# Cutting GpSimd's casts, products and masks into smaller instructions, together with a new order of the opening and fewer idle matrix products

## The chip, the cores and the metric

The kernel runs on one core of one Trainium2 chip. The metric is the device time of one execution in microseconds (us), and lower is better. A core has TensorE (PE in the profile; its weight loads are PEld), VectorE (DVE), ScalarE (ACT), GpSimd (POOL) and SyncE (SP), which here only starts transfers. In the traces the instructions of an engine run one after another (GpSimd's cast of q at 10.00 us stood behind that of a v tile at 9.42, though q was there at about 6.3, as the prediction works out), and the engines run beside each other (in the kernel before, PE, DVE, ACT and POOL are busy for 158.1, 144.6, 129.9 and 112.9 us of a span of 172.9). VectorE and GpSimd also hold each other up. In the kernel before, a cast of VectorE that takes 0.75 us elsewhere took 1.61 at 61.66, beside a cast of GpSimd, and GpSimd's next one 1.58 instead of 1.15. I call what VectorE's casts and masks wait for the port; that is a name for these waits.

## The reference, cut to what matters

```python
# q, k, v: (8, 8, 576, 64); w_in: (512, 1024); A_log: (512,); w_out: (512, 512)
scores = q @ k.transpose(0, 1, 3, 2) / sqrt(64)
scores = where(|i - j| <= 32, scores, -1e9)            # window of 65 positions
x = (softmax(scores) @ v)  -> (8, 576, 512)
val, gate = split(x @ w_in)                            # first projection
h[t] = exp(A_log)[0] * h[t-1] + val[t]                 # scan along the sequence
out = (silu(gate) * h) @ w_out                         # second projection
```

## The kernel before

Five strings (one for each engine) hold the order of the work as letters; further strings say which engine takes each shared piece. A small model of the engines assigns buffers, and `emit` writes the instructions. These are the parts that the change touches.

```python
SEQ = {"pe": "QKBmSKQSmSmSPPKtQVmSPPVm...", "pool": "vqkmavqwwwakwavvvmff...", ...}   # cut
SHARED = {"ck": "GDAGADGDGDGAGAGA", "mask": "pGppppGpDpppDpGpGDDDGD...", ...}        # G, D, A: the engine; cut

def keep_busy(seq, place, until):          # idle products: nobody reads their result
    ...
        n = int((o.start - max(at[b], 5.6 if first else 0.0) - (0.6 if first else 0.15))
                / (0.43 if first else 0.216))
    ...
# in emit(o), e being the engine of the piece
        elif kd in ("cq", "ck"):           # cast of a q or k tile, 128 x 1152, f32 -> f16
            copy(e, bf(n + "16", b, T).rearrange("p j y d -> p y j d"), bf(n, b, T))
        elif kd == "mask":                 # zero what lies outside the window, 128 x 1024
            for h in (slice(0, 2),) if e == "dve" else (slice(0, 1), slice(1, 2)):
                (nc.vector if e == "dve" else nc.gpsimd).tensor_tensor(
                    out=pr[:, h], in0=pr[:, h],
                    in1=m[:, None, :].to_broadcast([128, h.stop - h.start, 512]), op=ALU.mult)
        elif kd == "fuse":                 # silu(gate) * h, 128 x 512
            ...
                eng.tensor_tensor(out=bf("fu", c)[:, x, :], in0=bf("h", *key), in1=bf("si", *key), op=ALU.mult)
```

The softmax here doesn't subtract the row's maximum and nothing guards it: scores larger than these inputs give would overflow.

Of the kernel before, what the change touches and what calls it, by code (L numbers as in the profile page):

```python
# [10 lines left out]
ALU = mybir.AluOpType  # L11
# [6 lines left out]
HALVED = (0, 1, 8)  # L18
# [29 lines left out]
          "fev", "O": "out"}  # L48

SEQ = {  # L50
    "pe": "QKBmSKQSmSmSPPKtQVmSPPVmSQtKGGSmGSPPVVtGPPVGKtVGQGKFFQVmSSQVKFGFFmSPPmSmSSFPPtFKPPtK"
          "QVGmSSSVFGSPPGtVQtVGVPPKGQVQVSSSGFKFtGPPGFKtVSSPVGGQGKFSSPFFGPPSVQttVSSPFVKVQGFFFPSS"
          "VGPPFVQKGFVGPSSVGVVFGGQKVGPPPFFFSSSFFFFPPSVGVGPPVVGGtGGVVGVFGFFVFFFFFF",
    "act": "bvAExhxkxTexqxwxTEggxhvgxhhTkggwEwgegEooqxxevEoogoxxxovxoEvEevxgxxogqgxTTegvEgeexxgo"
           "xoEkggoEvxxqggegExoxooqxgeTkxoxEegvvoooxqgoxEgoegxgkxgogeEgovooxxooxooxggggggogogooo"
           "oo",
    "dve": "eqkavehEwrrnnEwhvhsrrnnwsesuvshurnrnssurnrnssuuTskusssuesvsssmvhvhurrnnkmrnrTnrnrTns"
           "hhsukrnrnuusmsurrnnsussmhmhuTrrnnuuTsrmnuusuvhhmrnrnrnsuTsrnsmsuvmhrhnsrurnnsusussru"
           "nsuusrnrvurnnhmmhmrnrmnsurrsnnususTususssussuussfoo",
    "pool": "vqkmavqwwwakwavvvmffwfqwfqffkvffkqvvmfmfqqvkvffvvmfffkvfmvvmfmfqffvvmkffmfqfmmfvffvv"  # L60
            "ffffffff",
    "sp": "LLLLLLLLLLLLLLLLLLLLLLLLLLLLLLLLLLLLLLLLLLLLLLLLLLLLLLLLLLLLLOLLLLLLLLOLLOLOOLLLLOLL"
          "OLOOOOOXOXLLOLOLLOLXXOOXOOOOOOOOOOOOOOOOOOO",
}
SHARED = {
    "cw": "DDGGDGAGGAAG",
    "ar": "DGGG",
    "ck": "GDAGADGDGDGAGAGA",
    "evk": "ADDAAAAAAAAAAAAA",
    "cq": "GDGAGGAGAGGAAGAG",  # L70
    "evq": "DDADADAAAAAAAAAA",
    "cv": "AGDGDDGGGAADDGDAAGGAAGGGGGAGGDGADAGGAGDG",
    "sh": "ADDDDAAADDDDDDDDDDDD",
    "mask": "pGppppGpDpppDpGpGDDDGDGDGGDDGGGGDDDD",
    "xe": "AAADDDAADDDAD",
    "fuse": "GGGGGGGGGGGGGGGGGGGGGGGGGGGGGGGGGGGD",
    "fev": "AAAAAAAAAAAAAAAAAAAAAAAAAAAAAAAAADAAD",
}
ORDER = ["q00", "v00", "a", "k00", "v01", "q01", "k01", "v02", "q10", "k10", "w00", "w02",
         "v03", "w01", "w03", "q11", "v04", "w11", "k11", "w12", "w10", "w13", "v10", "v11",  # L80
         "v12", "v14", "v13", "w23", "k20", "w20", "q20", "w21", "w22", "k21", "q21", "q30",
         "k30", "v21", "v23", "v20", "v22", "v24", "v30", "k31", "k40", "q31", "v31", "v32",
         "v33", "v34", "k41", "q40", "k50", "q50", "q41", "v40", "v41", "v42", "v51", "v43",
         "v44", "k51", "q61", "k60", "q51", "v52", "v50", "k61", "v53", "v54", "q60", "v63",
         "v62", "v60", "v61", "q70", "v64", "k70", "q71", "k71", "v74", "v72", "v70", "v71",
         "v73"]
ORDER = [(x[0],) + tuple(int(y) for y in x[1:]) for x in ORDER]


# [258 lines left out]
def keep_busy(seq, place, until):  # L348


    span, got = {}, {}
    for o in seq:
        for k in o.use:
            p, i = place[o.n, k]
            if p in ("ps1", "ps2"):
                lo, hi = span.get((k, i, p), (o.start, o.end))
                span[k, i, p] = min(lo, o.start), max(hi, o.end)
    t, first = 3.0, True
    for o in seq:
        if o.eng != "pe" or o.start > until or o.kind in ("mask", "ta") and first:  # L360
            continue
        at = [max([t] + [hi for (k, i, p), (lo, hi) in span.items()
                         if lo < o.start and (b == i or p == "ps2" and b == i + 1)]) for b in range(8)]
        b = min(range(8), key=lambda b: at[b])
        n = int((o.start - max(at[b], 5.6 if first else 0.0) - (0.6 if first else 0.15)) / (0.43 if first else 0.216))
        if n > 0:
            got[o.n] = [b] * n
        t, first = o.start + COST["pe", o.cost][0], False
    return got
# [3 lines left out]
def kernel(  # L373
# [10 lines left out]
    nc = tc.nc  # L384
# [21 lines left out]
    mask = T([128, 8, 64], f16, "mask")  # L406
# [56 lines left out]
    def two(ap):  # L463
        return ap.rearrange("p (i t) -> p i t", i=2)

    def emit(o):
# [49 lines left out]
        elif kd in ("cq", "ck"):  # L516
            b, T = key
            n = kd[1]
            copy(e, bf(n + "16", b, T).rearrange("p j y d -> p y j d"), bf(n, b, T))
        elif kd in ("trq", "trk"):  # L520
            b, T = key
            n = kd[2]
# [48 lines left out]
        elif kd == "mask":  # L571
            m = mask.rearrange("p r q -> p (r q)")
            pr = bf("pr", *key)
            for h in (slice(0, 2),) if e == "dve" else (slice(0, 1), slice(1, 2)):
                (nc.vector if e == "dve" else nc.gpsimd).tensor_tensor(  # L575
                    out=pr[:, h], in0=pr[:, h], in1=m[:, None, :].to_broadcast([128, h.stop - h.start, 512]), op=ALU.mult)
        elif kd == "pv":
            u, G = key
            pr, pv = bf("pr", *key), bf("pv", *key)
# [23 lines left out]
        elif kd == "xe":  # L603
            u, = key
            copy(e, bf("xT", u // 2)[:, u % 2].rearrange("p a t -> p (a t)"), bf("xt", u).bitcast(f16))
        elif kd == "xd":
            u, = key
            nc.sync.dma_start_transpose(out=bf("xT", u // 2)[:, u % 2].rearrange("p a (r t) -> p (a r) t", r=2),
                                        in_=bf("x16", u).rearrange("p a r h d -> p (a r h d)"))
        elif kd in ("pjv", "pjg"):  # L610
            c, x = key
            pj, xT, oc = bf(kd, *key), bf("xT", c), 0 if kd == "pjv" else 4
            if c in HALVED:
                parts = [(pj[:, 256 * i:256 * i + 256], oc + 2 * (x % 2) + i, 256 * (x // 2), 256) for i in range(2)]
            else:
                parts = [(pj, oc + x, 0, 512)]
            for to, w, t0, n in parts:
                for fc in range(4):
                    nc.tensor.matmul(out=to, lhsT=w_in16[:, fc, 128 * w:128 * w + 128],  # L619
                                     rhs=xT[:, t0 // 256:(t0 + n) // 256, fc, :], start=(fc == 0), stop=(fc == 3))  # L620
        elif kd == "scan":
            c, x, cc = key
            lo, n, t0 = (256 * (cc % 2), 256, 256 * (x // 2)) if c in HALVED else (0, 512, 0)
            before = prior(c, x, cc)
            init = bf("h", *before[0])[:, before[1]:before[1] + 1] if before else 0.0
            a0 = 512 - 64 * c + t0
            nc.vector.tensor_tensor_scan(out=bf("h", c, x)[:, lo:lo + n], data0=arep[:, cc, a0:a0 + n],  # L627
                                         data1=bf("pjv", c, x)[:, lo:lo + n], initial=init, op0=ALU.mult, op1=ALU.add)
        elif kd == "tanh":
            nc.scalar.activation(bf("th", *key), bf("pjg", *key), AF.Tanh, bias=0.0, scale=0.5)  # L630
        elif kd == "silu":
            nc.vector.scalar_tensor_tensor(out=bf("si", *key), in0=bf("th", *key), scalar=1.0,  # L632
                                           in1=bf("pjg", *key), op0=ALU.add, op1=ALU.mult)
        elif kd == "fuse":
            c, x = key
            eng = nc.gpsimd if e == "pool" else nc.vector
            if c in HALVED:
                i, t0 = 2 * (x % 2), 256 * (x // 2)
                eng.tensor_tensor(out=bf("fu", c)[:, i:i + 2, t0:t0 + 256], in0=two(bf("h", *key)), in1=two(bf("si", *key)),  # L639
                                  op=ALU.mult)  # L640
            else:
                eng.tensor_tensor(out=bf("fu", c)[:, x, :], in0=bf("h", *key), in1=bf("si", *key), op=ALU.mult)  # L642
        elif kd == "fin":
            c, tt = key[:2]
            cols = slice(256 * key[2], 256 * key[2] + 256) if len(key) > 2 else slice(0, 512)
            fo, fu = bf("fo", *key)[:, cols], bf("fu", c)
            for cc in range(4):
                nc.tensor.matmul(out=fo, lhsT=fu[:, cc, 128 * tt:128 * tt + 128],  # L648
                                 rhs=w_out16[:, cc, cols], start=(cc == 0), stop=(cc == 3))
        elif kd == "fev":  # L650
            cols = slice(256 * key[2], 256 * key[2] + 256) if len(key) > 2 else slice(0, 512)
            copy(e, bf("o", *key)[:, cols], bf("fo", *key)[:, cols])
        elif kd == "out":
            c, tt = key[:2]
            cols = slice(256 * key[2], 256 * key[2] + 256) if len(key) > 2 else slice(0, 512)
            r0 = 512 * c + 128 * tt
            nc.sync.dma_start(out=out_flat[r0:r0 + 128, cols], in_=bf("o", *key)[:, cols])
# [37 lines left out]
```

## Time and profile before

The median of three runs was 173.91 us (173.71 to 174.9). The profiled execution took 174.91, one us more than the median, for a span of 172.9.

| what | before |
|---|---|
| PE busy / GpSimd busy / GpSimd's instructions | 158.1 us / 112.9 us / 125 |
| one whole product on GpSimd (L642, L639) | 1.16 to 1.21 us |
| half a mask on GpSimd (L575) | 1.19 us |
| granted clock of TensorE | 1.00 in all slices; the clock records begin at 16.25 us |

The prediction below shows the busy row and the first three stages. The columns are the stretch, its length, and the busy us and number of instructions of PE, PEld, DVE, ACT and POOL, then granted clock, share of the DMA engines and GB/s.

### The profile page before, as it was taken

The page shows a single profiled execution, that of the slowest core. Times are in us where ns is not written, and L with a number is a line of the kernel's source. Part 1 is how long each engine was busy: PE and PEld are TensorE (multiplying, and loading weights), DVE is VectorE, ACT ScalarE, POOL GpSimd, SP SyncE. Part 2 cuts the span into 40 slices and gives each one's busy share as a digit, 9 for nine tenths or more (in the row PEclk, how much of TensorE's full clock was granted, in tenths as well). Part 3 has the DMA queues.
Part 4 walks back from the last instruction along what each step waited for, and adds up shares of the span by engine and source line. Part 5 has one row for each costly group of instructions (what it writes and reads, how often), then busy time and mean ns, then how long its engine had stood idle before and what let it go on. Part 6 is the DMA issues. An engine that isn't in the chain of part 4 may idle for free. (4 is left out here: it accounts for less than half of the span.)

```text
span 172.9 us, 5244 instructions
## 1 busy us (share of the span) xinstructions
PE 158.1 (91%) x2133; PEld 99.2 (57%) x2133; DVE 144.6 (84%) x237; ACT 129.9 (75%) x171; POOL 112.9 (65%) x125
## 2 busy tenths in 40 slices
PE   0949788998999998999999999999999999999991
PEld 0225466867967666566666565654654555458650
DVE  5117879988999999899999898979967997899970
ACT  3103849899899997999999999999696869522541
POOL 8560399669657192299949976992999990045520
PEclk9999999999999999999999999999999999999999
DMA  4999998999999979999899998991889428189155
GB/s 122 300 348 372 334 336 154 226 308 383 311 215 227 335 161 298 379 211 230 255 358 254 256 285 181 345 394 74 142 219 306 114 61 186 34 279 357 62 223 202
DMA packets 58574, 42.53 MB, mean 246 GB/s; under 512 B 44084, under 2 KB 44344, under 8 KB 58552
## 3 DMA queue, kind: packets, MB, share of 16 engines
q1 hardware_dynamic: 58552, 42.22, 84.8%
q8 instruction: 16, 0.26, 0.6%
q14 instruction: 6, 0.05, 0.1%
HBM read 31.46 MB, written 9.44 MB: 236 GB/s over the span
## 5 line engine op out<-in xcount | busy, mean ns | idle before, releaser
L619 PE MATMUL psum<-xT,w_in 128*128 128x256 f16 (+1 forms) x384 | 69.9, 326 | 0.4 <-ACT xT L449 0.4
L619 PEld LDWEIGHTS <-w_in 128*128 128x128 f16 x384 | 35.6, 98 | 21.0 <-issue 0.6
L627 DVE TENSOR_TENSOR_SCAN f2k<-arep,f2k,psum 128x512 f32<-128x512 f32 (+1 forms) x44 | 44.2, 1025 | 2.8 <-PE psum L619 2.7
L575 POOL TENSOR_TENSOR pr<-pr,mask 128x512 f16<-128x512 f16 x24 | 28.0, 1187 | 23.2 <-ACT pr L565 20.8
L565 ACT ACTIVATE pr<-psum 128x1024 f16<-128x1024 f32 x36 | 36.4, 1028 | 3.5 <-PE psum L560 3.2
L642 POOL TENSOR_TENSOR fu<-f2k,si 128x512 f16<-128x512 f32 x24 | 28.9, 1214 | 13.2 <-DVE rc L590 9.0
L648 PE MATMUL psum<-w_out,fu 128*128 128x512 f16 (+1 forms) x148 | 34.6, 373 | 0.1
L630 ACT ACTIVATE th<-psum 128x512 f16<-128x512 f32 x36 | 21.5, 605 | 8.7 <-PE psum L619 7.2
L449 ACT ACTIVATE f2k<-psum 128x512 f32<-128x512 f32 (+1 forms) x35 | 20.2, 604 | 9.9 <-PE psum L648 8.4
L632 DVE SCALAR_TENSOR_TENSOR si<-th,psum 128x512 f16<-128x512 f16 x36 | 23.8, 674 | 3.5 <-ACT th L630 3.2
L595 DVE TENSOR_TENSOR x<-psum,rc 128x512 f16<-128x512 f32 x36 | 23.8, 680 | 0.5
L648 PEld LDWEIGHTS <-fu 128*128 128x128 f16 x148 | 13.9, 98 | 13.7
L639 POOL TENSOR_TENSOR fu<-f2k,si 128x512 f16<-128x512 f32 x11 | 12.7, 1159 | 10.3 <-DVE si L632 6.5
L449 ACT ACTIVATE kT<-psum 128x1152 f16<-128x1152 f16 x14 | 15.9, 1138 | 2.1 <-PE psum L525 2.1
L662 PE MATMUL psum<-eye,ident 128*128 128x512 f16 x34 | 12.1, 491 | 5.3 <-POOL eye L434 4.2
L456 POOL TENSOR_SCALAR vE<-v 128x512 f16<-128x512 f32 x20 | 12.7, 643 | 4.2 <-DMA v<-in_v_dram 4.0
L586 PEld LDWEIGHTS <-pr 128*64 128x64 f16 x576 | 11.5, 111 | 6.5 <-issue 5.2
L449 ACT ACTIVATE qT<-psum 128x1152 f16<-128x1152 f16 x12 | 13.7, 1140 | 0.6 <-PE psum L525 0.5
L525 PE MATMUL psum<-ident,q 128*128 128x128 f16 x144 | 11.2, 225 | 3.0 <-POOL q L456 3.0
L560 PEld LDWEIGHTS <-kT 64*128 64x128 f16 x576 | 10.5, 95 | 5.8 <-issue 4.1
L586 PE MATMUL psum<-vO,pr 128*64 128x65 f16 x256 | 13.1, 197 | 0.8 <-DVE vO L452 0.5
L586 PE MATMUL psum<-vE,pr 128*64 128x65 f16 x320 | 13.6, 197 | 0.2
(65 smaller groups left out, 195.9 us busy)
## 6 DMA issues: line engine op xcount, KB each, us to landing
stg<-in_q_dram SPq DMA_DIRECT2D x16, 576.0 KB, 8.3
stg<-in_k_dram SPq DMA_DIRECT2D x16, 576.0 KB, 6.6
out_dram<-f2k SPq DMA_DIRECT2D x35, 256.0 KB, 3.8
v<-in_v_dram SPq DMA_DIRECT2D x24, 256.0 KB, 6.5
v<-in_v_dram SPq DMA_DIRECT2D x16, 192.0 KB, 5.1
f2k<-in_moe_w_in_dram SPq DMA_DIRECT2D x8, 256.0 KB, 8.8
f2k<-in_moe_w_out_dram SPq DMA_DIRECT2D x4, 256.0 KB, 7.0
out_dram<-f2k SPq DMA_DIRECT2D x2, 128.0 KB, 1.9
```

Source lines behind the costliest of these rows:

```text
L449: nc.scalar.activation(dst, src, AF.Copy, bias=0.0, scale=mul)
L456: nc.gpsimd.tensor_scalar(out=dst, in0=src, scalar1=mul, scalar2=1.0, op0=ALU.mult, op1=ALU.mult)
L565: nc.scalar.activation(bf("pr", *key), bf("sc", *key), AF.Exp, bias=0.0, scale=1.0 / 8.0)
L575: (nc.vector if e == "dve" else nc.gpsimd).tensor_tensor(out=pr[:, h], in0=pr[:, h], in1=m[:, None, :].to_broadcast([128, h.stop - h.start ...
L586: nc.tensor.matmul(out=pv[p0:p0 + 64, h, x0:x0 + 65], lhsT=pr[:, h, at:at + 64], rhs=vt, start=True, stop=True)
L595: nc.vector.tensor_tensor(out=x, in0=view[:, :, :, 0:64], in1=bf("rc", *key)[:, :, :, None].to_broadcast([128, 2, 4, 64]), op=ALU.mult)
L619: nc.tensor.matmul(out=to, lhsT=w_in16[:, fc, 128 * w:128 * w + 128], rhs=xT[:, t0 // 256:(t0 + n) // 256, fc, :], start=(fc == 0), stop=( ...
L627: nc.vector.tensor_tensor_scan(out=bf("h", c, x)[:, lo:lo + n], data0=arep[:, cc, a0:a0 + n], data1=bf("pjv", c, x)[:, lo:lo + n], initial ...
L630: nc.scalar.activation(bf("th", *key), bf("pjg", *key), AF.Tanh, bias=0.0, scale=0.5)
L632: nc.vector.scalar_tensor_tensor(out=bf("si", *key), in0=bf("th", *key), scalar=1.0, in1=bf("pjg", *key), op0=ALU.add, op1=ALU.mult)
L642: eng.tensor_tensor(out=bf("fu", c)[:, x, :], in0=bf("h", *key), in1=bf("si", *key), op=ALU.mult)
L648: nc.tensor.matmul(out=fo, lhsT=fu[:, cc, 128 * tt:128 * tt + 128], rhs=w_out16[:, cc, cols], start=(cc == 0), stop=(cc == 3))
```

## The change

It has three parts. GpSimd's q and k casts and its products are issued as two instructions and its masks as four; the intention was that VectorE, where it has to wait at the port, waits for a shorter instruction. The order of the work is new; the opening is what it was meant to speed up, but the strings differ to their ends. And fewer idle products are issued.

```diff
 SEQ = {
-    "pe": "QKBmSKQSmSmSPPKtQVmSPPVmSQtKGG..."
+    "pe": "mQBKQKKSSSmSQPPmmSPSPKttVVmQmV..."        (all five strings, SHARED and ORDER: cut)
-        n = int((o.start - max(at[b], 5.6 if first else 0.0) - (0.6 if first else 0.15)) / (0.43 if first else 0.216))
+        n = int((o.start - max(at[b], 5.6 if first else 0.0) - (0.6 if first else 0.3)) / (0.43 if o.start < 20.0 else 0.216))
@@ cast of q and k
-            copy(e, bf(n + "16", b, T).rearrange("p j y d -> p y j d"), bf(n, b, T))
+            to, src = bf(n + "16", b, T).rearrange("p j y d -> p y j d"), bf(n, b, T)
+            for y in (slice(0, 1), slice(1, 2)) if e == "pool" else (slice(0, 2),):
+                copy(e, to[:, y], src[:, y])
@@ mask
             for h in (slice(0, 2),) if e == "dve" else (slice(0, 1), slice(1, 2)):
+                for x in (slice(0, 512),) if e == "dve" else (slice(0, 256), slice(256, 512)):
@@ product
+            for i in (slice(0, 2),) if e == "dve" else (slice(0, 1), slice(1, 2)):
+                ...
+                eng.tensor_tensor(out=to, in0=two(h)[:, i], in1=two(si)[:, i], op=ALU.mult)
```

## The prediction

> **What bounds the kernel now.** I read the page's busy row first, then the table of busy time by stage, the same table for the idle products alone (L662, matrix products whose result nobody reads[...]), then the chain of waits, then the timelines of GpSimd, TensorE and VectorE around the places that those pointed to. The first fence is the page's busy row and the stage table (columns: stretch, its length, then busy us of PE, PEld, DVE, ACT, POOL); the second is the stage table of L662 alone.
>
> ```profile
> PE 158.1 (91%) x2133; PEld 99.2 (57%) x2133; DVE 144.6 (84%) x237; ACT 129.9 (75%) x171; POOL 112.9 (65%) x125
> 0.00:16.50 16.50, 9.71 (x39) 4.27 (x41) 6.65 (x23) 3.31 (x5) 8.54 (x21) 1.00 0.90 284
> 16.50:30.00 13.50, 11.17 (x220) 7.79 (x220) 10.55 (x17) 10.01 (x10) 9.77 (x12) 1.00 1.03 280
> 30.00:75.00 45.00, 43.34 (x725) 31.60 (x722) 42.57 (x68) 41.62 (x55) 27.26 (x30) 1.00 0.98 283
> 75.00:169.30 94.30, 93.87 (x1167) 55.52 (x1159) 84.47 (x131) 74.92 (x103) 67.30 (x64) 1.00 0.77 219
> ```
>
> ```profile
> 0.00:16.50 16.50, 7.15 (x16) 2.08 (x16) 1.00 0.90 284
> 16.50:30.00 13.50, 3.50 (x14) 1.22 (x13) 1.00 1.03 280
> 30.00:75.00 45.00, 1.42 (x5) 0.36 (x5) 1.00 0.98 283
> 75.00:169.30 94.30, 0.00 (x0) 0.00 (x0) 1.00 0.77 219
> ```
>
> TensorE is the bound. Its useful work is about 158.1 - 12.1 = 146.0 us, and it ends at 169.3, so 23.3 us of TensorE's time are lost, all of it idle or spent on idle products. By stage the loss is 16.5 - (9.71 - 7.15) = 13.9 us before 16.5, then 13.5 - (11.17 - 3.50) = 5.8, then 45 - (43.34 - 1.42) = 3.1, then 0.4. From 75 us to the end nothing can be won except by arriving there with more work done. After 169.3 an eviction and the last transfer take the remaining 3.6 us of the 172.9 us span; the timed run is about 1 us above the span. The chain of waits agrees: from 121.9 us on it is TensorE alone.
>
> ```profile
> 121.91 1.02 PE psum L648 x4
> ...
> 164.89 4.34 PE psum L648 x24
> 169.23 0.02 issue
> 169.25 0.42 DVE f2k L452
> ```
>
> So the change is worth what it takes from the 19.7 us lost before 30 us and from the 3.1 us after them. Why is the opening slow? The next fence is GpSimd's timeline, the one after it TensorE's.
>
> ```profile
> 9.42 0.62 POOL L456 TENSOR_SCALAR vE<-v 128x512 f16<-128x512 f32 x1 [2.62 <-DMA v<-in_v_dram]
> 10.00 1.15 POOL L456 TENSOR_SCALAR q<-stg 128x1152 f16<-128x1152 f32 x1
> 11.12 1.15 POOL L456 TENSOR_SCALAR k<-stg 128x1152 f16<-128x1152 f32 x1
> ```
>
> ```profile
> 11.21 1.14 PE L525 MATMUL psum<-ident,q 128*128 128x128 f16 x9 [2.59 <-POOL q L456]
> 14.84 1.72 PE L662 MATMUL psum<-eye,ident 128*128 128x512 f16 x4
> 16.48 0.41 PE L560 MATMUL psum<-qT,kT 64*128 64x64 f16 x16
> ```
>
> The first q tile was asked for before the first v tile, and ScalarE took that v at 6.29, so q was there at about 6.3; yet its cast began at 10.00, because GpSimd runs in order and stood in front of a v tile until 9.42. That is 3.7 us lost at the very start. Also, ScalarE had the first kT out at 14.53 + 1.12 = 15.65, but the first scores started at 16.48: the idle products before them, 0.43 us each at the slow clock, overran by 0.8 us.
>
> The second subject is the port. The next fence is VectorE's timeline at 60 us, then GpSimd's.
>
> ```profile
> 61.66 1.61 DVE L452 CAST k<-stg 128x1152 f16<-128x1152 f32 x1
> 63.20 1.62 DVE L575 TENSOR_TENSOR pr<-pr,mask 128x1024 f16<-128x1024 f16 x1
> ```
>
> ```profile
> 61.51 1.15 POOL L456 TENSOR_SCALAR k<-stg 128x1152 f16<-128x1152 f32 x1
> 62.70 1.58 POOL L456 TENSOR_SCALAR q<-stg 128x1152 f16<-128x1152 f32 x1
> ```
>
> The cast of 0.75 us (as at 13.67) took 1.61, ending 0.6 after GpSimd's instruction ended at 62.66; the mask of 0.69 took 1.62, ending half a us after GpSimd's next.
>
> [...] Here nine transposes took 1.14 at 11.21 and 0.68 at 16.82, so the clock came up some 5.5 us after work began[...]; the granted-clock column reads 1.00 throughout and does not show this.
>
> **The change part by part.**
> Counting letters in the diff, TensorE's useful instructions are the same: 146 us stay. VectorE gets two more masks, one more shift, one more arep and one more q cast, and loses two k casts, two weight casts and a v cast: 2 x 0.69 + 0.7 + 0.7 + 0.75 - 2 x 0.75 - 2 x 0.42 - 0.42 = +0.8 us. ScalarE gets four q/k casts and one weight cast more, three v casts and one shift less: 4 x 1.17 + 0.63 - 3 x 0.63 - 1.07 = +2.3 us on an engine 75% busy.
>
> Splitting: GpSimd's casts took 0.622 us for 512 elements and 1.152 for 1152, a slope of 0.83 ns and a fixed part of about 0.2 us; back to back, starts are 0.04 closer than durations, so a cut costs about 0.16 us (I take the same for products). Cuts: 35 products, 13 casts, 10 masks with two each, 68 in all, x 0.16 = +10.9 us. The moved work is two masks (-4.5), three q casts (-3.5), one arep (-1.2), four v casts (+2.3) and one weight cast (+0.6) = -6.3. GpSimd goes from 112.9 to about 117.5 us, 68%: still not a bound. A product comes 0.16 us later; in the last stage it is followed by TensorE work that is already queued, so little of it reaches the end.
>
> What the cuts give: I added, over VectorE's timeline, how much each cast, shift or mask exceeded its usual 0.42, 0.75, 0.70 or 0.69. Fifteen were long, by 6.6 us in all, 2.5 of it between 25 and 33 us. Waits end with GpSimd's current instruction, so halved instructions should about halve them: 3.3 us of VectorE back. Nearly all of this falls beside a TensorE that is already full after 75 us. Before that, TensorE has 3.1 us to regain between 30 and 75; I allow 0.5, and charge 0.3 for the later products.
>
> The opening: k, q, k, q, k, q now come first and v afterwards. In 3.13 us (6.29 to 9.42) 832 KB landed, 272 GB/s. The first q is now second in the queue, behind a k: 576 + 576 KB where before 576 + 192 KB were in at 6.29, so it lands near 7.5. VectorE casts it (0.75), TensorE transposes at about 8.3, against 11.21. ScalarE then evicts it (1.13), and only after that casts the first k (1.17), which I read from its order; transpose (1.1) and VectorE's eviction (1.36) put the first kT at about 14.5. Two more k halves are transposed before the scores, so these start at about 16, close to 16.48, but with three scores in a row. v and the weights land later: up to the fourth first-projection weight the old order has 5.4 MB in front, the new one 6.5, some 3 us more, so 24.5 against about 21. The first projection was at 26.65; following the engines by hand I get 26.3. Before it the new order has one k transpose (0.5), two scores (0.8), two products with v (0.86), one x transpose (0.45) and a mask (0.2) more: 2.8 us of useful work that the old order did later. I count 2.0 of it, because this hand schedule assumes that each landing is on time. The overrun of the idle products, 0.8, is inside this.
>
> Sum: -2.0 - 0.5 + 0.3 = -2.2 us, and 173.9 - 2.2 = 171.7; fewer idle products late in the opening may add 0.2. I say 171.5.
>
> **The rivals.**
> First: the opening is limited by DMA and the lead evaporates. For it: the DMA share is 1.03 from 16.5 to 30[...]. Then projections wait and the time is 173 to 174. Against it: the attention work that can run meanwhile is there.
> Second: VectorE becomes the bound after 30 us. It was busy 42.57 of 45 there, so a TensorE 2.5 us ahead may wait for it. That eats the lead: 173. Against it: [...]there are 10 us of slack after 75.
> Third: everything works, and the 3.1 us between 30 and 75 go too: 2.8 + 2 us, 169.2.
> Fourth: fewer idle products let the clock fall again in the opening[...]. Against it: useful products are denser.
>
> **Range and chances.** The first two rivals are real but only take back a gain, the third is what a good search would reach. Range 169.2 to 173.9. Two per cent faster is 170.4, which needs about 3.5 us of the at most 5: 0.28. Two per cent slower is 177.4, which needs a new stall after 75 us: 0.04. Within: 0.68.
>
> **What would show it.** The first transposes should start near 8.3, the first scores near 16, the first projection near 26, and the loss up to 30 us should fall from 19.7 to about 17.5. Stage 75 to the end should stay full. GpSimd's half products should take about 0.68 us and its busy time be near 117; VectorE's long casts and masks should sum to 3 to 4 us. I am wrong if TensorE shows gaps after 75 us, if the loss between 30 and 75 grows by over 1 us, or if the opening's loss does not fall.

What no trace of this case shows is cut from it, and no term of its sum is among the cuts: -2.0 - 0.5 + 0.3 = -2.2 us, so 171.7, and 171.5 with the idle products. "Waits end with GpSimd's current instruction" generalizes the two waits that it shows (1.61 and 1.62 us) and is tested below. That fewer idle products let the clock fall, its fourth rival, isn't shown.

## More of the kernel before

```profile
75.00:95.00 20.00, 19.89 (x268) 12.39 (x261) 19.46 (x32) 18.92 (x25) 17.58 (x18) 1.00 0.99 261
95.00:130.00 35.00, 34.76 (x507) 20.18 (x506) 30.05 (x45) 32.94 (x43) 29.19 (x28) 1.00 0.85 238
130.00:150.00 20.00, 20.00 (x237) 10.55 (x236) 17.31 (x28) 15.34 (x23) 12.42 (x13) 1.00 0.58 138
```

TensorE is full. The fifth busy figure is the one to keep in mind: GpSimd, 65% busy on average, is busy for 46.8 of the 55 us from 75 to 130.

The two costliest groups of GpSimd's instructions, from the page (line, engine, operation, tiles, count | busy us, mean ns | idle before):

```profile
L575 POOL TENSOR_TENSOR pr<-pr,mask 128x512 f16<-128x512 f16 x24 | 28.0, 1187 | 23.2 <-ACT pr L565 20.8
L642 POOL TENSOR_TENSOR fu<-f2k,si 128x512 f16<-128x512 f32 x24 | 28.9, 1214 | 13.2 <-DVE rc L590 9.0
```

## The result, and the profile after

The changed kernel took 181.75 us (181.33 to 182.14, four runs) against 174.41 of the kernel before in the same rounds: a ratio of 1.042, with a 95% interval of 1.035 to 1.048. It is slower. A ratio in this text is the mean time of one kernel's fast runs over that of the other's of the same rounds, so it is not quite the ratio of the medians that stand beside it. A run is labelled slow when it is over 1.5% above the fastest run of its kernel, and fast otherwise; ratios use fast runs alone.

First the busy row of the page and the stages after, with the columns explained above.

```profile
PE 158.7 (88%) x2112; PEld 99.0 (55%) x2112; DVE 150.3 (83%) x238; ACT 132.9 (74%) x172; POOL 120.6 (67%) x189
0.00:16.50 16.50, 10.16 (x86) 6.04 (x87) 7.95 (x24) 6.78 (x8) 9.67 (x24) 1.00 0.90 271
16.50:30.00 13.50, 10.45 (x188) 7.47 (x188) 11.37 (x21) 11.63 (x14) 4.35 (x7) 0.87 1.06 296
30.00:75.00 45.00, 42.88 (x695) 30.56 (x693) 40.20 (x69) 41.18 (x52) 29.06 (x42) 1.00 1.05 291
75.00:95.00 20.00, 17.93 (x238) 10.65 (x236) 18.61 (x27) 16.83 (x22) 18.06 (x29) 1.00 0.91 243
95.00:130.00 35.00, 34.80 (x511) 20.24 (x510) 32.50 (x47) 31.50 (x43) 31.59 (x47) 1.00 0.85 249
130.00:150.00 20.00, 15.64 (x179) 8.11 (x176) 17.29 (x20) 9.86 (x16) 13.86 (x23) 0.91 0.35 105
```

The gaps are where the prediction said that it would be wrong: 2 us of TensorE's time are lost between 75 and 95 and 4.4 between 130 and 150, where the kernel before lost 0.1 and nothing. In that last stage the granted clock fell to 0.91 as well.

The opening did most of what was expected. From TensorE's timeline after (start, us, engine, line, operation, tiles; in brackets the idle time before it and what ended it):

```profile
7.51 1.14 PE L527 MATMUL psum<-ident,q 128*128 128x128 f16 x9 [0.70 <-DVE q L452]
15.22 0.70 PE L562 MATMUL psum<-qT,kT 64*128 64x64 f16 x32
28.54 1.91 PE L623 MATMUL psum<-xT,w_in 128*128 128x256 f16 x16 [0.41 <-DVE xT L452]
```

The first transposes start at 7.51, against 11.21, and the first scores at 15.22, against 16.48. The first projection, though, starts at 28.54, later than before (26.65). To follow the lead I gave every useful matrix product its time at full clock and subtracted the sum of those that had started from the time. This is my own reckoning from the traces; it doesn't count work at half clock as more work, as a sum of busy times does. Done again with slightly other weights, it gives the same within 0.5 us up to 50 us and within about 1.6 us later. Positive numbers are us by which a kernel is ahead of the profiled execution of the kernel before; the experiments in the other columns come below.

| at (us) | after | order only | one drain | cut before 65 | before, cut before 65 | before, cut and drained |
|---|---|---|---|---|---|---|
| 16.5 | 2.3 | 2.3 | 2.3 | 2.3 | 1.0 | 0.0 |
| 30 | 1.6 | 2.7 | 2.5 | 1.7 | 1.4 | -0.2 |
| 50 | 2.1 | 3.5 | 3.1 | 2.4 | 1.4 | 0.0 |
| 75 | 0.7 | 0.5 | 2.1 | 1.6 | 1.5 | 0.3 |
| 95 | -0.8 | 1.0 | 0.5 | 1.8 | 1.8 | -1.4 |
| 130 | -0.6 | 0.7 | 0.3 | 1.3 | 1.3 | -1.9 |
| 140 | -4.6 | 0.7 | 0.0 | 1.9 | 2.5 | -2.6 |
| 150 | -5.9 | 0.3 | 0.1 | 1.1 | 1.6 | -3.1 |
| 165 | -7.8 | 0.4 | 0.0 | 1.7 | 2.4 | -4.6 |

The changed kernel holds a lead of about 2 us up to 50, loses it by 95, and loses 4 us more at once between 135 and 140. This is VectorE's timeline there, after:

```profile
132.91 1.28 DVE L631 TENSOR_TENSOR_SCAN f2k<-arep,f2k,psum 128x512 f32<-128x512 f32 x1 [0.17 <-PE psum L623]
134.10 5.27 DVE L578 TENSOR_TENSOR pr<-pr,mask 128x1024 f16<-128x1024 f16 x1
139.30 1.27 DVE L631 TENSOR_TENSOR_SCAN f2k<-arep,f2k,psum 128x512 f32<-128x512 f32 x1
```

And GpSimd's, in the same stretch:

```profile
133.78 1.29 POOL L648 TENSOR_TENSOR fu<-f2k,si 128x256 f16<-128x256 f32 x2
135.04 2.53 POOL L578 TENSOR_TENSOR pr<-pr,mask 128x256 f16<-128x256 f16 x4
137.54 1.28 POOL L648 TENSOR_TENSOR fu<-f2k,si 128x256 f16<-128x256 f32 x2
```

A mask that takes 0.69 us took 5.27. Seven of GpSimd's instructions followed the one that ran when VectorE asked, so seven ends of an instruction passed before VectorE had its turn. The mask ended 0.55 us after GpSimd had nothing more to do, at 138.82. The next scan stood behind the mask, and TensorE behind the scan:

```profile
132.71 3.62 PE L623 MATMUL psum<-xT,w_in 128*128 128x512 f16 x16
140.62 1.18 PE L623 MATMUL psum<-xT,w_in 128*128 128x512 f16 x4 [4.29 <-DVE f2k L631]
```

Four products take 1.18 us after the gap and about 0.9 at full clock (16 took 3.62). The page's row of granted clock, 40 slices of 4.5 us in tenths, shows why:

```profile
PEclk9999699999999999999999999999999699999999
```

The second 6 is the slice from 139.7 us; in the trace's clock records the clock is 0.5 from 141.35 to 144.76. That is 3.41 us at half rate, or 1.7 us lost on top of the 4.29. TensorE had stood still for 4.29 us, and had run again for 0.73 us when the clock fell; with one drain (below), which has no such gap, this fall is missing. The first 6 is another stretch of half clock, 18.47 to 21.88, again 3.41 us. No such gap came before it: in the 3.4 us ahead of it TensorE's longest pause was 0.82 us. So what makes the clock fall isn't shown.

The groups of GpSimd, to be read beside those of before:

```profile
L648 POOL TENSOR_TENSOR fu<-f2k,si 128x256 f16<-128x256 f32 x70 | 47.9, 708 | 17.0 <-DVE si L636 16.9
L578 POOL TENSOR_TENSOR pr<-pr,mask 128x256 f16<-128x256 f16 x40 | 26.3, 689 | 16.8 <-ACT pr L567 16.8
```

The size of the halves was predicted well: 0.71 and 0.69 us with their waits, 0.66 at the least.

### The profile page after: what moved, and what is told of

It reads as the page before. It is cut to its first block, busy times and chain, and to the rows that moved or that the text cites. A ratio compares the mean times of both kernels' runs of the same rounds, so it can differ in the third digit from the quotient of the medians.

```text
span 180.3 us, 5270 instructions
## 1 busy us (share of the span) xinstructions
PE 158.7 (88%) x2112; PEld 99.0 (55%) x2112; DVE 150.3 (83%) x238; ACT 132.9 (74%) x172; POOL 120.6 (67%) x189
## 4 chain that ended last, share of the span: by engine, by line
PE 34%; DVE 24%; DMA 14%; POOL 12%; issue 8%; ACT 4%; SPq 2%; DVEq 0%; ACTq 0%; POOLq 0%
PE psum L623 17%; DMA v<-in_v_dram 9%; DVE f2k L631 8%; PE psum L654 8%; POOL pr L578 6%; PE psum L527 3%; POOL fu L648 3%; PE psum L590 3%; DVE si L636 3%; DVE pr L578 3%; DMA stg<-in_q_dram 3%; DMA xT<-x 2%; DVE vO L452 2%; DVE vE L452 2%; PE psum L605 2%
## 5 line engine op out<-in xcount | busy, mean ns | idle before, releaser
L648 POOL TENSOR_TENSOR fu<-f2k,si 128x256 f16<-128x256 f32 x70 | 47.9, 708 | 17.0 <-DVE si L636 16.9
L578 POOL TENSOR_TENSOR pr<-pr,mask 128x256 f16<-128x256 f16 x40 | 26.3, 689 | 16.8 <-ACT pr L567 16.8
L654 PE MATMUL psum<-w_out,fu 128*128 128x512 f16 (+1 forms) x148 | 36.3, 381 | 0.4 <-DVE x L599 0.4
L456 POOL TENSOR_SCALAR vE<-v 128x512 f16<-128x512 f32 x24 | 16.1, 679 | 10.0 <-DMA v<-in_v_dram 9.8
L449 ACT ACTIVATE qT<-psum 128x1152 f16<-128x1152 f16 x13 | 14.6, 1130 | 8.3 <-PE psum L527 8.3
L449 ACT ACTIVATE kT<-psum 128x1152 f16<-128x1152 f16 x13 | 14.7, 1134 | 7.2 <-PE psum L527 7.2
L578 DVE TENSOR_TENSOR pr<-pr,mask 128x1024 f16<-128x1024 f16 x15 | 16.7, 1119 | 0.6 <-ACT pr L567 0.3
L590 PE MATMUL psum<-vE,pr 128*64 128x65 f16 x320 | 14.3, 197 | 2.3 <-DVE pr L578 1.5
L594 DVE RECIPROCAL rc<-psum 128x8 f32<-128x8 f32 x36 | 7.0, 199 | 8.4 <-PE psum L590 8.2
L527 PE MATMUL psum<-ident,k 128*128 128x128 f16 x144 | 12.5, 241 | 1.6 <-ACT k L449 0.8
```

What stands on the lines that cost most here:

```text
L449: nc.scalar.activation(dst, src, AF.Copy, bias=0.0, scale=mul)
L527: nc.tensor.transpose(out=t[:, 128 * j:128 * j + 128], in_=s[:, j].rearrange("p y d -> p (y d)"), identity=ident)
L578: (nc.vector if e == "dve" else nc.gpsimd).tensor_tensor(out=pr[:, h, x], in0=pr[:, h, x], op=ALU.mult, in1=m[:, None, x].to_broadcast([12 ...
L590: nc.tensor.matmul(out=pv[p0:p0 + 64, h, x0:x0 + 65], lhsT=pr[:, h, at:at + 64], rhs=vt, start=True, stop=True)
L648: eng.tensor_tensor(out=to, in0=two(h)[:, i], in1=two(si)[:, i], op=ALU.mult)
L654: nc.tensor.matmul(out=fo, lhsT=fu[:, cc, 128 * tt:128 * tt + 128], rhs=w_out16[:, cc, cols], start=(cc == 0), stop=(cc == 3))
```

## The experiments

The theory: the cut instructions let VectorE starve at the port. (To starve is to wait past several ends of GpSimd's instructions, which the expectations call boundaries; the hole is TensorE's gap of 4.29 us.) Rivals: the new order brings the hole by itself; the idle products let the clock fall; the halves cost by their longer total.

### The change with whole instructions

```diff
-            for y in (slice(0, 1), slice(1, 2)) if e == "pool" else (slice(0, 2),):
+            for y in (slice(0, 2),):                  # and the same for masks and products
```

> The changed kernel with all of GpSimd's instructions whole again, new order and new idle products kept. Theory S (the halves let a back-to-back GpSimd keep the port past several boundaries): no VectorE instruction waits over 1.5 us for the port, the 4.3 us hole of TensorE near 136 us and the slow-clock window after it go, time 173 to 175. Rival O (the new order puts that mask in front of a run of GpSimd work, whole or halved): a mask of 4 us or more stays, time 180 or more. Rival I (idle products): the slow window near 18 us stays in both cases.

It took 174.56 us against 173.62, ratio 1.005 (0.999 to 1.011). No VectorE wait exceeded its usual duration by more than 1.01 us, and there is no hole near 136 (column "order only"). So the new order with the new idle products is not what costs 7 us; cutting is. The clock didn't fall near 18 us here, so rival I's slow window, expected in both cases, is missing. But the order alone also brings nothing to the end: its lead, 3.5 us at 50 and 3.0 at 55, is down to 1.0 at 60, after three waits of VectorE at the port of some 0.83 us each, at 55.7, 57.0 and 58.6.

### The kernel before with all of GpSimd's instructions cut

```diff
+            for y in (slice(0, 1), slice(1, 2)) if e == "pool" else (slice(0, 2),):   # likewise masks, products
```

> The kernel before with the halves alone, its own order and idle products. Theory S: at least one VectorE instruction that waits past several GpSimd boundaries, long waits summing to 8 us or more, time 176 to 182. Rival O: waits fall to 3 to 4 us, time 173 to 175.

Its five runs gave 177.66 to 180.58 us, median 178.22, and the fast ones a ratio of 1.022 (1.015 to 1.029), of class unclear. Its profile is of a run labelled slow (180.44); no fast run was profiled. There a cast of VectorE, 0.42 us otherwise, took 3.31 us at 140.80 and passed four ends of an instruction. Cutting makes the old order slower too, since the interval lies above 1.

### Only the products cut

```diff
-            for y in (slice(0, 1), slice(1, 2)) if e == "pool" else (slice(0, 2),):
+            for y in (slice(0, 2),):                  # masks likewise; products stay halved
```

> The changed kernel with only the products h*silu in halves; masks and casts whole. In the long wait of the changed kernel, boundaries between products, between masks and from one to the other were all missed. Theory S, any short instruction: a long wait can still come, 175 to 181. If it is the halved masks in particular: none, 173 to 175. Rival O: 180 or more.

It took 176.11 us (173.98 to 177.52), ratio 1.009 (1.001 to 1.017). The profile, again of a run labelled slow, has three long waits at 86.1 to 91.1 (1.48 to 1.65 us), of which only the first passed more than one end of an instruction, and the clock at half from 92.6 to 96.0. The wait of 5 us is absent.

### The old number of idle products

```diff
-        ... - (0.6 if first else 0.3)) / (0.43 if o.start < 20.0 else 0.216))
+        ... - (0.6 if first else 0.15)) / (0.43 if first else 0.216))
```

> The changed kernel with the idle products' two constants of before. Theory S: no slow-clock window near 18 us, up to 1.7 us better in the opening, but the hole near 136 us stays: 179 to 182. Rival I (fewer idle products are the main cause): 175 or less.

182.77 us, ratio 1.051 (1.044 to 1.059). The half-clock stretch at 18 us went away, and the time didn't fall. That the old number removed it isn't shown: five of the other versions with the new number (whole, products only, three whole, both with drains) have no such stretch either, and the kernel before, cut before 65, has one from 11.65 to 15.07 with the old number. The hole is the same: the mask at 134.31 took 5.28 us. The idle products aren't the cause.

### The port by itself, short runs (wrong result)

```python
for s in range(STEPS):                                   # VectorE asks a little later each time
    for i in range(4): for j in range(cuts):
        if gap: nc.gpsimd.memset(tiny, 0.0)
        nc.gpsimd.tensor_tensor(out=fu[...], in0=h[...], in1=si[...], op=mult)   # back to back
    nc.vector.tensor_copy(fill[:, 0:900 + 48 * s], psum)                         # a delay
    nc.vector.tensor_tensor(out=pr, in0=pr, in1=mask, op=mult)                   # asks
```

> Wrong result on purpose: the wait measured by itself. 96 trials, each: GpSimd does four 512-wide products back to back, VectorE first copies 900 to 2004 columns out of PSUM (in steps of 48) and then wants the port. Sets of 24: halves against a mask, whole products against a mask, halves with a tiny memset in front of each, halves against a cast. Theory S, halves miss boundaries whatever else runs: in the sets with halves some trials wait past the first boundary, up to the end of GpSimd's run (1.3 us or more), with whole products none waits over 1.2 us. Rival: the length makes no difference, waits end at the first boundary in all sets. If the tiny memset opens the port, no wait over 0.7 us in that set.

In 96 trials, VectorE asking during the 2nd to 7th instruction of the run, every wait, also in the 24 trials with tiny memsets in between, ended at the first end of a GpSimd instruction: at most 1.18 us for a mask between halves, 1.68 between whole ones. Here the prediction's rule holds, so small size alone isn't what starves VectorE.

### Casts and masks cut, products whole

```diff
-            for i in (slice(0, 2),) if e == "dve" else (slice(0, 1), slice(1, 2)):
+            for i in (slice(0, 2),):                  # products whole
```

> The changed kernel with masks and casts in parts and the products whole. Theory S: the run at 134 us still holds four quarter masks, so the wait may end at the boundary of a whole product or last to the end of the masks: 174 to 181. With the run with only the products halved (176.1 us) it tells which of the two holds the port.

180.9 us, ratio 1.045 (1.035 to 1.054); the mask at 131.70 took 4.85 us. So the products need not be cut for the long wait to come.

### The changed kernel with the three pieces beside that mask whole

```diff
+ masks:    ... if e == "dve" or key == (15, 1) else ...
+ products: ... if e == "dve" or key in ((5, 3), (6, 0)) else ...
```

> The changed kernel with three of GpSimd's operations whole again, those that ran while VectorE's mask waited from 134 to 139 us: products (5,3) and (6,0), mask (15,1). Theory S: that mask waits 1.2 us at most, TensorE's 4.3 us hole and the slow window after it go, 174.5 to 177. Rival O: the long wait stays, 181 or more. If the loss is spread over the halves: 180 or more with the wait gone.

180.08 us, ratio 1.042 (1.031 to 1.052). The mask still waited, 4.70 us at 132.44, through four whole instructions. So whole instructions, run while VectorE waited, didn't end this wait. What is left is what it ran before.

### How long GpSimd has run without a break (wrong result)

```python
for us in (2, 5, 8, 11, 13, 15, 18, 21, 24):             # GpSimd's run before VectorE asks
    for i in range(int((us + 7.5) / (1.115 if cuts == 1 else 0.63))):
        nc.gpsimd.tensor_tensor(...)                     # halves or wholes, back to back
    # VectorE: copies from PSUM as a delay, then a mask or a cast
```

> Wrong result on purpose. In eight runs of the kernels every wait that missed more than one boundary came after GpSimd had run without a pause for 13.6 to 20.4 us (18 to 33 instructions); all waits after shorter runs ended at the first boundary. Here GpSimd runs products back to back and VectorE, which until then only copies out of PSUM, asks for the port 2 to 24 us after the run began (9 delays, 4 phases each; halves and a mask, whole products and a mask, halves and a cast). Theory R (after a long unbroken run GpSimd isn't interrupted any more): up to some 12 us the wait ends at the first boundary, from some 14 us on it lasts to the end of the run (about 7 us). Rival: the wait ends at the first boundary for every delay, and something in the kernel other than the length of the run is needed.

I count GpSimd's instructions from the start of the unbroken run up to the one under way when VectorE asked. Between halves, a mask asked for during the 5th to 11th took at most 1.18 us; during the 16th or later (8.93 us into the run) it took 6.82 us at first and in every case lasted to the end of the run. Between wholes the change came between the 14th (14.49 us in; the mask took 0.68) and the 15th (14.66 us in; 6.06). A cast can starve too: in the kernel before with all cut, one took 3.31 us instead of 0.42. In time the two limits differ, 6 to 9 us for halves and 14.5 for wholes; as a count of instructions they may be the same.

### The changed kernel with GpSimd drained after every eighth instruction

```diff
+        if o.eng == "pool":
+            if run >= 8:
+                nc.gpsimd.drain()
+                run = 0
+            run += {"mask": 4, "fuse": 2, "cq": 2, "ck": 2}.get(o.kind, 1)
```

> The changed kernel with a drain in GpSimd's program before the next operation once 8 instructions have gone by since the last, so that its runs are broken. Theory R: no wait of VectorE over 1.2 us, the hole at 134 us and its slow window go, 174 to 177 with what the drains cost. Rival: the 4 to 5 us wait stays, 180 or more.

175.85 us (175.37 to 177.06), ratio 1.014 (1.009 to 1.019). No wait of VectorE exceeded 1.21 us; the mask, now at 133.21, took 1.10. The clock stayed at 1.00. Drains, which do no work, gave back nearly 6 us by the medians (181.75 - 175.85), and about 4.9 by the ratios (1.042 and 1.014, each against the kernel before in its own rounds).

### The count, pinned down (wrong result)

```python
SETS = [("half", 9..15), ("quarter", 8, 12, 16, 22), ("whole", 12, 14),
        ("drain", 18), ("twice", 20), ("tiny", 8, 11), ("sem", 18)]
# drain: one in the middle; twice: a first mask in the middle; tiny: a memset of one element
# after each half; sem: one product waits for a semaphore that ScalarE has long set
```

> Wrong result on purpose. VectorE asks with a mask after a known number of GpSimd instructions run back to back, two phases of each. Theory (GpSimd keeps the port once some 14 instructions have been queued back to back, whatever their length): halves give up the port at the first boundary after 9, 10, 11 and 12 instructions (the mask takes at most 1.2 us) and keep it to the end of the run after 15 (some 7 us); quarters of 0.4 us each, which reach 16 instructions in only 6.4 us, keep it at 16 and 22 and give it up at 8 and 12; wholes give it up at 12 and keep it at 14. Rival (time, not count): quarters give it up in all four cases, since 22 of them last only 8.4 us. A drain in the middle starts the count anew: after 18 halves with a drain at the tenth, the mask waits for one boundary only. A mask that wins the port in the middle does so too (the second mask after 20, with a first after 10, waits one boundary), and so would a semaphore wait in the middle[...]; this last I hold for open, 50 to 50. Tiny memsets between halves count as instructions: 8 pairs (16) keep the port, as 11 pairs do; if only long ones count, both give it up.

VectorE's timeline of this run: the last trial that gets the port, and the first that doesn't. Both asked for the same mask.

```profile
85.20 0.78 DVE L60 TENSOR_TENSOR pr<-pr,mask 128x1024 f16<-128x1024 f16 x1
100.51 6.38 DVE L60 TENSOR_TENSOR pr<-pr,mask 128x1024 f16<-128x1024 f16 x1
```

The first was asked for during the 14th instruction of GpSimd's run (a small copy and then halves), the second during the 15th of its run, 8.74 us after its start.

VectorE asked two to five instructions later than the numbers in SETS say, counted so, so some sets that should have given up the port (halves and wholes at 12, one of the two trials of quarters at 12) kept it. I go by the count in the trace. All forms together, counted in the same way:

| GpSimd's run | asked during the | the mask took (us) |
|---|---|---|
| halves, 0.65 us | 12th, 13th, 14th | 0.78 to 1.13 |
| halves | 15th to 19th | 6.03 to 6.38 |
| quarters, 0.4 us | 10th, 14th (5.06 us in) | 0.80 to 1.04 |
| quarters | 15th (5.23 us in) to 26th | 7.02 to 7.44 |
| wholes, 1.15 us | 15th (15.1 us in) to 17th | 5.14 to 5.62 |
| halves, drained in the middle | 22nd | 0.87, 1.03 |
| halves, a mask in the middle got the port | 25th | 0.80, 1.26 |
| halves with tiny memsets between | 20th to 28th | 0.68 to 1.19 |
| halves, a satisfied wait in the middle | 22nd | 5.61, 5.78 |

It is a count here, not a time: with quarters the change comes at 5.1 to 5.2 us, with halves at 8.1 to 8.7, always between the 14th and the 15th instruction. A drain clears the count (the mask took 0.87 and 1.03 us at the 22nd instruction; in the kernels' traces a drain leaves GpSimd idle for 0.16 to 0.18 us where it waits for nothing else), and so does a turn of VectorE (0.80 and 1.26 at the 25th); a wait that is already satisfied doesn't (5.61 and 5.78). I had expected the tiny memsets to count; instead they break the run (at most 1.19 us up to the 28th). What the count comes from, the runs don't show.

In the kernels' traces, where I count GpSimd's instructions since its last pause or VectorE's last turn at the port, the starved mask of the changed kernel was asked for during the 18th: VectorE had last used the port for the mask at 121.49, and from then until 134.10 GpSimd never paused. In the kernels' traces I found thirteen waits that passed more than one end of an instruction: eleven at counts of 16 to 32, and two at 12, which the count doesn't explain. Two at 18, in the kernel before at 139.53 and in a version of it, still ended at the first end. I can't say why.

### The changed kernel, cut only in the first part

```diff
-            for y in (slice(0, 1), slice(1, 2)) if e == "pool" else (slice(0, 2),):
+            for y in (slice(0, 1), slice(1, 2)) if e == "pool" and o.start < 65.0 else (slice(0, 2),):
```

> The kernel after with GpSimd's instructions cut only where the schedule's model has them start before 65 us, whole after that. Theory (count of GpSimd's back-to-back instructions): no VectorE wait over 2 us and no hole near 140, the lead of the opening (about 2 us) held to 65 and mostly lost after it: 172 to 175 us, ratio 0.99 to 1.01. Rival (the new order is bad in the second half in any case): 178 us and over with a hole near 135 to 145 though the instructions there are whole.

Masks and products are cut under the same condition. 172.96 us (172.47 to 174.33) against 173.7, ratio 1.000 (0.994 to 1.007). No wait over 1.71 us, no hole. Against the version with whole instructions throughout (174.56, of another job), cutting the first part may gain 1.6 us; by the ratios it is 0.8 and the intervals overlap, so this isn't shown. Against the changed kernel, not cutting the rest saves 8.8 us by the medians and about 7.2 by the ratios. The clock was at half here too, from 18.31 to 21.72.

### The kernel before, cut only in the first part

```diff
+ the same condition, o.start < 65.0, in the kernel before with its own order
```

> The kernel before, its order and its idle products, with GpSimd's instructions cut only where the model starts them before 65 us. Theory: none of the long wait that the kernel before had with all of them cut (3.31 us at 141), some of the 1.2 to 1.5 us kept by which that one led at 65 to 85: 172.5 to 174, ratio 0.99 to 1.00. Rival (cutting costs by itself, by its longer total): 175 and over.

172.39 us (172.14 to 173.26), ratio 0.995 (0.990 to 1.000). It beats the changed kernel by 8 to 9 us; whether it beats the kernel before is not resolved.

### The changed kernel with one drain

```diff
+        if o.n == 706:            # GpSimd's product after the two masks that end at 128.7
+            nc.gpsimd.drain()
```

> The kernel after with one drain on GpSimd, after the two masks that end 5 us before VectorE's starved mask near 134; nothing else changed. Theory: the mask then comes after 8 to 10 instructions and takes under 1.4 us; the lag behind the kernel before stays near the 0.6 to 1.0 us that the kernel after showed at 130 to 135, no stretch of half clock near 141, and the time is 174 to 176.5 us (ratio 1.00 to 1.015), so one instruction gives back 5 us or more. Rival (the order is to blame for the hole, or the starving only moves on): the mask or a later one waits over 3 us, and the time stays over 179.

175.57 us (174.46 to 177.04) against 173.67, ratio 1.012 (1.007 to 1.016). VectorE's timeline at the mask:

```profile
132.51 0.89 DVE L578 TENSOR_TENSOR pr<-pr,mask 128x1024 f16<-128x1024 f16 x1
```

One instruction gives back 181.75 - 175.57 = 6.2 us by the medians of two jobs, or about 5.2 by the ratios, 1.042 and 1.012. The trace of the changed kernel had 4.29 of idle time and 1.7 of half clock at that mask, 6.0 together. This part is closed: of the 7.3 us that the change cost, this one wait is the most, 5 to 6 us.

### The kernel before, all cut, drained after every eighth

```diff
+        if o.eng == "pool":       # as above, in the kernel before with cut instructions
```

> The kernel before with all of GpSimd's instructions halved and a drain ahead of an operation once eight have gone since the last. Theory: the cast that took 3.31 us near 141 takes under 1.2, the lead of some 1.2 us at 65 to 85 lasts to the end, 172 to 173.5 us (ratio 0.99 to 1.00; the whole-in-the-later-part version had 172.39). Rival (the halves are slower for their own longer total, 0.16 us for each cut): 175 and over.

179.1 us (178.01 to 179.64), ratio 1.030 (1.026 to 1.033). My theory missed here, and the rival's figure (175 and over) held. Starving was indeed gone: the cast took 0.88 us, at 143.32, and no wait passed more than one end of an instruction. The chain of waits of this run, from 126 to 147 us, is GpSimd alone, but for short issue steps and drains that waited while GpSimd worked (start, us, engine, tile and line):

```profile
129.03 2.50 POOL pr L578 x4
...
134.26 1.27 POOL fu L648 x2
135.53 2.51 POOL pr L578 x4
...
140.80 1.25 POOL fu L648 x2
```

And the busy times of that stretch, in the order PE, PEld, DVE, ACT, POOL; of this run, then of the kernel before:

```profile
126.00:147.00 21.00, 19.49 (x249) 10.76 (x246) 16.53 (x23) 15.27 (x22) 20.30 (x33) 1.00 0.66 166
```

```profile
126.00:147.00 21.00, 21.00 (x285) 11.24 (x283) 17.42 (x27) 17.32 (x25) 16.42 (x16) 1.00 0.71 174
```

GpSimd is busy for 20.3 of 21 us where it was busy for 16.4: it has become the bound there. So the cuts have a second cost, their own length, where GpSimd is nearly full. The drains have a part in it that no run separates: there are twenty, and GpSimd is idle for 0.16 us or more at each. The same cuts without drains had taken 177.66 to 178.22 us in their fast runs, so no gain from ending the starving shows in this kernel.

## Why the prediction was wrong

The time predicted was 171.5 us, with a range up to 173.9; 181.75 came. Point by point:

- **The opening (-2.0 us): right in size, in this pair of profiles, but one of its signs missed.** The lead of useful work was 2.3 us at 16.5 and 1.6 to 2.1 from 30 to 50, against 2.0 counted. The first transposes came at 7.5 (8.3 predicted), the first scores at 15.2 (16), but the first projection at 28.5 (26.3). The sum of losses by stage, which the prediction offered as a check, would have flattered it: after, it is 9.5 us up to 16.5 (16.5 - 10.16 + 3.13 of idle products) and 14.8 up to 30, where about 17.5 was predicted, since more of the busy time there is transposes at the slow clock (nine in 1.14 us at 7.51, against 0.68 at 16.82 in the kernel before).
- **A reading that was off, and on which no term rests: "the clock came up some 5.5 us after work began".** TensorE had begun at 4.20 us with ten idle products, which took 4.42 us, 0.44 each, about twice the 0.23 of the products of that size at full clock (16 in 3.62), so at about half rate. The trace's clock records begin at 16.25, at full clock, 12 us after that and 5.0 after the first transposes.
- **GpSimd's durations: right.** A cut costs 0.14 us (two halves start 0.63 apart, against 1.12 for a whole), 0.16 predicted; GpSimd's busy time is 120.6 us, against 117.
- **"Waits end with GpSimd's current instruction, so halved instructions should about halve them: 3.3 us of VectorE back": this step failed.** In the runs the first half of that sentence holds only up to the 14th instruction of an unbroken run (a mask took 0.78 us); from the 15th on, VectorE waits for the run's end (6.38; but for the four waits of the kernels' traces named above). Halved instructions are more for the same work, 189 instead of 125 on GpSimd, so the limit is met sooner. VectorE's waits rose from 6.6 us in 15 to 11.3 in 17. One of them, 4.6 us over the usual 0.69, cost 5 to 6 us of the result, which the run with one drain shows. Even without it the sum wasn't halved: 6.2 us in 15 waits with one drain, 6.2 with a drain after every eighth. The two parts of the kernel differ, though. Before 65 us the step held: in the kernel before the waits fell from 5.1 us to 1.9 when that part was cut. After 65 us they grew: from 1.5 us to 4.6 in the kernel before with cuts and drains, and from 3.0 with whole instructions to 4.4 with one drain in the new order.
- **"68%: still not a bound. A product comes 0.16 us later ... little of it reaches the end": failed as well, with the smaller size.** With one drain the changed kernel still takes 175.57, and 172.96 if its later part isn't cut: 2.6 us by the medians, 2.0 by the ratios, for the cuts after 65 us, with the big wait gone. Draining throughout doesn't lower it (175.85). In the kernel before the same cuts, with twenty drains, made GpSimd the bound for 20 us, which its chain shows, and cost 179.1 - 172.4 = 6.7 us with no starving left. That the 2.6 us of the new order are of the same kind is only argued: from 75 to 95 TensorE is busy for 17.9 us with the cuts and for 20.0 when only the part before 65 is cut, GpSimd for 18.1 and 17.2, but one wait there, at 86.90, also passed two ends of an instruction.
- **The rivals.** VectorE as the bound (the second) came nearest, but as a full stop of VectorE at one place, not as a lack of slack. A fall of the clock in the opening (the fourth) is in the trace at 18 us, but it isn't shown that fewer idle products bring it, and putting them back gained nothing; the fall that cost time came after the hole. A slowdown of over 2% had 4 chances in 100, because the prediction had no way for a wait to grow beyond one instruction.
- **What remains when nothing is cut after 65 us is the new order and the first part's cuts.** This kernel is at 172.96, not resolved from the kernel before. The profiled execution of the kernel before was 1 us longer than its median, so the leads of the table are about 1 us too large against a typical one.

In sum, with medians of different jobs, in which the kernel before took 173.67 to 174.41: 181.75 - 6.2 (the starved mask) - 2.6 (the other cuts after 65) = 172.95, which is 1.5 us above the prediction. This sum can't fail, since its last term was taken from the kernel cut only before 65, whose median it gives back. By the ratios the two terms are about 5.2 and 2.0. Where the last 1.5 us went stays open.

## What to carry to other kernels

Count the instructions that GpSimd issues without a pause ahead of each VectorE instruction that waits for it (here casts and masks). Cutting them shortened a single wait, from at most 1.68 us for a mask between whole products to 1.18 between halves, but it brings forward the point (here the 15th instruction, where the mask took 6.38 us against 0.78 at the 14th) from which VectorE mostly got no turn until the run ended. Where long runs can't be avoided, try a drain on GpSimd ahead of the point: here it ended the run (the mask of the changed kernel took 0.89 us instead of 5.27), and drains left GpSimd idle for 0.16 to 0.18 us where it waited for nothing else. And read the load of an engine by stage before lengthening its work: 65% on average was 78% of the stretch where it mattered, and 97% with cuts and drains.
